# Attention and routed experts in one kernel: a new numbering of the expert arms, list scatters moved behind copies, one load of the first step, and small blocks that scatter without a copy

## The chip, the cores and the metric

The kernel runs on one core of a Trainium2 chip. The metric is device time in microseconds, from one launch to its end. Five engines work side by side: TensorE (PE; its weight loads are listed as PEld), VectorE (DVE), ScalarE (ACT), GpSimd (POOL) and SyncE (SP), the last of which mostly issues DMAs. Each has its own instruction stream, and they wait for each other by semaphores.

## The reference, cut to what matters

```python
# attention: 8 batches, 12 heads, 448 positions, 64 wide
scores = scale * np.matmul(q, k.transpose(0, 1, 3, 2)) - np.log(S)
attn = 1.0 / (1.0 + np.exp(-scores))
attn_out = np.matmul(attn, v)
x = attn_out.transpose(0, 2, 1, 3).reshape(B * S, H * D)      # 3584 x 768
# experts: only tokens with a positive skip score, one of 8 experts each
do_compute = x @ w_skip > 0
logits = x[do_compute] @ w_gate;  e_idx = argmax(logits)
y = gate_w * (relu(x @ w1[e]) @ w2[e])                        # 768 -> 1024 -> 768
out = x;  out[do_compute] += y
```

## The kernel before, in words

**Attention.** A step is one batch `b` and one pair of heads `hp`; there are 8 x 6 = 48 steps, and each has four chunks `c` of key positions. For a chunk PE makes scores (L217) into a PSUM tile of the tag s, of which there are two, ACT makes the sigmoid (L237) into a tile `at`, and PE multiplies with v (L245) into the PSUM tile `pa` of the step. PE's order is scores of chunk c, then values of chunk c − 2. The operands of the scores come from 32 x 32 block transposes on DVE (L202, `prep`). For those, a head pair's keys and queries lie in SBUF twice, the second time 32 rows lower and shifted by 32 columns. `load_kq` (L177) loads one such part by DMA, and `other_part` (L184) makes the second by copies on POOL, four for each two steps; they are in POOL's stream at c = 0 of each even step and fill the tiles of the two steps after it. The first step is special: `kq_first` is loaded in both parts, by eight DMAs from SP's and ACT's queues. PE multiplies an identity meanwhile (L594, `keep_busy`).

**Routing.** Three steps into a batch, the tokens of the batch before are assigned to experts, and a token's record is written to its expert's list in DRAM by an indirect DMA from POOL (L394), four per batch. They are kept in the list `due`, from which one is taken at set places in the order that is written out by hand: at steps hp = 3 after chunks 1 and 3, and at hp = 4 between and behind the copies of `other_part`. In the last batch two are taken at hp = 2, the others at hp = 3 after chunks 0 and 1. POOL also computes low parts of weights (L466) in the later batches.

**Experts.** Two blocks of 128 tokens of one expert are written out (`b0`, `b1`). Then a loop on the device (L1493) runs over the rest, with one kind of block each, read from a table. Two compares (L1482, L1483, L1488 in `choose`) lead into one of four arms: FULL (128 tokens), HALF (64), FEW (32) and SPLIT, which is FULL and splits the raw weights of the next expert into high and low parts on ACT and DVE besides. With these inputs the loop runs 14 times: SPLIT, HALF, FULL, HALF, FULL, then FEW and FULL twice, FEW, SPLIT, FEW, FULL, FEW. Each engine has the code of all four arms in its stream, one behind the other.

In FEW, a matmul has only 32 rows of output, so four quarters share PE: output half `o` (of two, 384 columns each) and inner half `m`. All four lie in one PSUM tile, `py`. ACT evicts those with m = 0 (L1400), DVE adds those with m = 1 (L1402). Then `put` has POOL test the sums (`seen`, L1253, which reads two elements), copy both halves from `yt` to `ys` (L1262), test again, and add the rows to the output by an indirect DMA (L550).

Of the kernel before, what the change touches and what calls it, by code (L numbers as in the profile page):

```python
# [10 lines left out]
F32 = mybir.dt.float32  # L11
# [8 lines left out]
P = 128  # L20
# [3 lines left out]
def kernel(  # L24
# [183 lines left out]
    def scores(b, hp, c, xs):  # L208

        sc = new_s(f"s_{b}_{hp}_{c}")
        for m in range(2):
            first, qs = (4 * m + c, slice(0, S)) if c < 3 else (3, slice(m * HQ, (m + 1) * HQ))
            for j in range(2):
                r = slice(j * D, (j + 1) * D)
                nc.tensor.matmul(  # L217
                    sc[m * D : (m + 1) * D, j, : qs.stop - qs.start],
                    xs[r, 0, first::NR7],
                    xs[r, 1, qs],  # L220
                    start=True,
                    stop=True,
                )
        return sc
# [346 lines left out]
    kq0 = wk.tile([P, 2, 1, NJ * D], F32, tag="xt", name="kq_first")  # L571
    for n in range(2):
        for h, eng in enumerate((nc.sync, nc.scalar)):
            load_kq(kq0, 0, 0, slice(0, 1), range(ND), (n,), (h,), eng)
    kq = {0: new_kq(0, 0)}
    load_kq(kq[0], 0, 0, slice(1, 2), range(1))

    warm = const.tile([P, 1], F32, name="warm")
    nc.scalar.activation(warm, bias, AF.Sigmoid)
    vs = {0: load_v(0, 0, 2)}  # L580
    kq[1] = new_kq(*steps[2])
    load_kq(kq[1], *steps[2], slice(0, 2), range(1))
# [62 lines left out]
    for n, (b, hp) in enumerate(steps):  # L645
# [39 lines left out]
        for c in range(4):  # L685
# [3 lines left out]
            if c == 0 and n % 2 == 0 and n + 2 < N:  # L689
                for g in range(2):  # L690
                    other_part(kq[n // 2 + 1], g)
                    if due and hp == 4 and b < B - 1:
                        due.pop(0)()
            if c == 0 and nxt:
                xs_next = prep(*nxt, part(n + 1)[0])
            done = next_values() if len(line) == 2 else None
# [32 lines left out]
                        wsplit(*w)  # L729


            if due and hp == 3 and (c % 2 if b < B - 1 else c < 2):
                due.pop(0)()

            if c == 3 and ready and not (hp == (3 if b < B - 1 else 2) and b > 0) or c == 1 and waiting:
# [263 lines left out]
    V.tensor_tensor(lnb, af, f_p, op=ALU.add)  # L999

    V.memset(f_hf, 0.0)
    V.tensor_scalar(f_last, f_last, 0.0, float(SPLIT), op0=ALU.is_gt, op1=ALU.mult)
# [245 lines left out]
    def put(n):  # L1248

        pool.tensor_tensor(rp[0], rid[:, 0:1], zero, op=ALU.add)  # L1250
        pool.tensor_tensor(rs, rp[0], zero, op=ALU.add)
        def seen(y, at):
            pool.tensor_tensor(  # L1253
                jk[:n], y[:n, at - 1 : at + 1], y[:n, at - 1 : at + 1], op=ALU.add
            )

        if n == SM:

            for o in range(2):
                seen(yt, (o + 1) * H2 - 1)  # L1260
                s = slice(o * H2, (o + 1) * H2)
                pool.tensor_copy(ys[:n, s], yt[:n, s])  # L1262
# [78 lines left out]
    def few(i):  # L1341
# [50 lines left out]
        for g in range(4):  # L1392
            load_w2(g, nx)
        for m in range(2):
            for o in range(2):
                g = 2 * o + m
                s = slice(o * H2, (o + 1) * H2)
                p = py[g * SM : (g + 1) * SM, 0, :H2]
                if not m:
                    nc.scalar.activation(yt[:SM, s], p, AF.Copy, scale=recs[:SM, 0, 0:1])  # L1400
                    continue
                nc.vector.scalar_tensor_tensor(  # L1402
                    yt[:SM, s], p, recs[:SM, 0, 0:1], yt[:SM, s], op0=ALU.mult, op1=ALU.add
                )
# [3 lines left out]
    def half(i):  # L1408
# [58 lines left out]
        advance()  # L1467

    arms = {
        FULL: lambda i: block(i, False),  # L1470
        SPLIT: lambda i: block(i, True),
        HALF: half,
        FEW: few,
    }
# [6 lines left out]
    def choose(kind, i):  # L1481
        with tc.If(kind < HALF) as c:  # L1482
            with tc.If(kind < FEW) as d:  # L1483
                run(FULL, i)
            with d.Else():
                run(FEW, i)
        with c.Else():
            with tc.If(kind < SPLIT) as d:  # L1488
                run(HALF, i)
            with d.Else():  # L1490
                run(SPLIT, i)

    with tc.For_i(0, nreg, 1, iteration_sync="reg_based") as i:  # L1493
        kind = entry(TYP, ds(i + 2, 1), mybir.ALL_ENGINES, SPLIT)
        choose(kind, i)


# [26 lines left out]
```

## Time and profile before

| | us |
|---|---|
| runs | 531.62, 535.46, 537.47 (median 535.46) |
| profiled execution | 538.86 |
| its span | 537.2 |
| PE busy | 506.3 |
| DVE busy | 296.9 |
| ACT busy | 274.0 |
| POOL busy | 259.5 |
| first scores on PE | 7.63 |
| loop's first matmul | 327.77 |
| last matmuls of the loop begin | 518.47 |
| last indirect DMA issued on POOL | 526.73 |

The profiled execution takes 1.66 us more than its span, and 3.4 us more than the median of the runs. The span falls into attention (to about 287 us), the routing's end with the two blocks written out (to about 325 us), and the loop. In the rows of the timeline stand the start, the length, the engine, the line, the operation with what it writes and reads, the count, and in brackets the idle time of the engine before it and what ended that. A "q" behind an engine's name is its sequencer, which reads instructions ahead of the engine's work and takes the branches.

### The profile page before, as it was taken

The numbers are of one execution on the slowest core, as the hardware profiler recorded it, in microseconds if no ns is written. First come the engines' busy times: TensorE is split into PE (matmuls) and PEld (weight loads), VectorE is DVE, ScalarE is ACT, GpSimd is POOL, SyncE is SP. The second block draws the span as 40 slices with busy tenths as digits, with TensorE's granted clock in tenths as the row PEclk, the third lists the DMA queues.
The fourth block names the chain that finished last, engine by engine and source line by source line (L and its number), as shares of the span: only waits on it lengthen the run. The fifth ranks groups of instructions, "written<-read, shape, count | busy, mean of one in ns | idle before, by whom it ended". The sixth has DMA issues, their size and how long they took to land.

```text
span 537.2 us, 15241 instructions
## 1 busy us (share of the span) xinstructions
PE 506.3 (94%) x4985; PEld 337.0 (63%) x4986; DVE 296.9 (55%) x732; ACT 274.0 (51%) x483; POOL 259.5 (48%) x413
## 2 busy tenths in 40 slices
PE   7999999999999999999999998999999999999970
PEld 5555555555555555556446986859587878787850
DVE  4555758568586795675856922962213232369321
ACT  3676766767767566666662122922212323177220
POOL 3523554345566874666674140453324444455642
PEclk8999999999999999999999998999999999999995
DMA  7999897798999899998964046688493959595930
GB/s 207 202 232 221 174 200 152 153 185 176 206 207 233 191 212 197 192 224 168 216 111 95 1 128 245 227 246 299 128 380 108 378 165 381 175 393 163 366 75 7
DMA packets 140481, 107.67 MB, mean 200 GB/s; under 512 B 97013, under 2 KB 112795, under 8 KB 140432
## 3 DMA queue, kind: packets, MB, share of 16 engines
q1 hardware_dynamic: 134096, 97.88, 70.0%
q0 software_dynamic: 4576, 8.66, 7.1%
q8 instruction: 31, 0.51, 0.4%
q10 hardware_dynamic: 1760, 0.48, 0.4%
q14 instruction: 18, 0.15, 0.1%
HBM read 98.93 MB, written 17.60 MB: 217 GB/s over the span
## 4 chain that ended last, share of the span: by engine, by line
PE 74%; DMA 9%; DVE 4%; SPq 4%; issue 3%; ACT 2%; POOL 1%; ACTq 0%; POOLq 0%; DVEq 0%
PE s L217 16%; PE pa L245 14%; PE ph L496 12%; PE py L523 11%; DMA out_dram<-y 4%; PE b_ph L496 3%; PE b_py L523 3%; PE py L1347 3%; PE ph L1347 3%; SPq L268 2%; PE pxt L472 2%; PE py L1414 2%; PE ph L1414 2%; DVE x L202 1%; DMA wr<-in_moe_w_dram 1%
## 5 line engine op out<-in xcount | busy, mean ns | idle before, releaser
L237 ACT ACTIVATE at<-s,bias 128x896 f32<-128x896 f32 x192 | 172.0, 914 | 84.6 <-PE s L217 82.3
L217 PE MATMUL s<-x 64*64 64x448 f32 (+1 forms) x1536 | 166.1, 501 | 7.0 <-DVE x L202 3.3
L245 PE MATMUL pa<-at,v 64*64 64x448 f32 (+1 forms) x1536 | 162.2, 490 | 0.0
L184 POOL COPY kq<-kq 32x896 f32<-32x896 f32 (+1 forms) x96 | 88.2, 919 | 104.6 <-DMA kq<-in_q_dram 62.0
L217 PEld LDWEIGHTS s<-x 64*64 64x64 f32 x1536 | 79.0, 191 | 63.7 <-issue 26.4
L245 PEld LDWEIGHTS pa<-at,v 64*64 64x64 f32 x1536 | 62.0, 133 | 55.7 <-issue 47.6
L202 DVE STREAM_TRANSPOSE x<-kq 128x448 f32<-128x448 f32 x94 | 83.0, 945 | 13.7 <-POOL kq L184 11.8
L255 DVE TENSOR_TENSOR xt<-xt,pa 128x448 f32<-128x448 f32 x48 | 29.5, 614 | 46.1 <-ACT xt L642 42.3
L394 POOL DMA_INDIRECT lst<-rec,idx x32 | 32.3, 1009 | 18.3 <-issue 10.5
L466 POOL TENSOR_TENSOR wl<-wr,wh 128x384 fp32r<-128x384 f32 (+1 forms) x28 | 31.7, 1143 | 8.9 <-DVE wh L465 7.7
L260 DVE STREAM_TRANSPOSE y<-xt 128x448 f32<-128x448 f32 x48 | 31.0, 646 | 4.4 <-DMA out_dram<-y 2.6
L550 POOL DMA_INDIRECT out_dram<-ys,rp x15 | 23.7, 1578 | 15.8 <-issue 8.2
L505 ACT ACTIVATE hs<-ph 128x512 f32<-128x512 f32 x14 | 8.4, 598 | 43.9 <-PE ph L496 35.9
L523 PE MATMUL py<-wh,hh 128*128 128x384 f32 x112 | 29.8, 346 | 0.0
L516 DVE TENSOR_TENSOR hl<-pht,hh 128x512 fp32r<-128x512 f32 x14 | 9.7, 690 | 36.0 <-ACT hh L515 27.6
L523 PE MATMUL py<-wh,hl 128*128 128x384 f32 x112 | 28.8, 338 | 0.0
L523 PE MATMUL py<-wl,hh 128*128 128x384 f32 x112 | 28.7, 337 | 0.0
L496 PE MATMUL ph<-wh,xh 128*128 128x512 f32 x84 | 26.3, 410 | 2.6 <-issue 2.6
L496 PE MATMUL ph<-wl,xh 128*128 128x512 f32 x84 | 27.2, 410 | 0.0
L482 DVE TENSOR_TENSOR xl<-pxt,xh 128x384 fp32r<-128x384 f32 x30 | 15.3, 552 | 20.7 <-PE py L1347 8.9
L642 ACT ACTIVATE xt<-pa 128x448 f32<-128x448 f32 x48 | 25.7, 536 | 1.9 <-PE pa L245 1.3
L496 PE MATMUL ph<-wh,xl 128*128 128x512 f32 x84 | 25.2, 404 | 0.0
(273 smaller groups left out, 666.9 us busy)
## 6 DMA issues: line engine op xcount, KB each, us to landing
raw<-in_moe_w_dram SPq DMA_DIRECT2D x64, 768.0 KB
v<-in_v_dram SPq DMA_DIRECT2D x48, 256.0 KB
out_dram<-y SPq DMA_DIRECT2D x192, 56.0 KB
kq<-in_k_dram SPq DMA_DIRECT2D x46, 224.0 KB
kq<-in_q_dram SPq DMA_DIRECT2D x46, 224.0 KB
wr<-in_moe_w_dram SPq DMA_DIRECT2D x12, 256.0 KB
wr<-in_moe_w_dram SPq DMA_DIRECT2D x16, 192.0 KB
lst<-fill SPq DMA_DIRECT2D x4, 464.0 KB
```

The costliest lines, as they stand in the source:

```text
L184: nc.gpsimd.tensor_copy(a[BT:, :, :, :BT], a[:BT, :, :, BT:])
L202: nc.vector.transpose(xs[:, n].rearrange("p (r j) -> p j r", j=NJ), t.rearrange("p (j d) -> p j d", d=D)[:, :, :BT],)
L217: nc.tensor.matmul(sc[m * D : (m + 1) * D, j, : qs.stop - qs.start], xs[r, 0, first::NR7], xs[r, 1, qs], start=True, stop=True,)
L237: nc.scalar.activation(at[:, :, :n], sc[:, :, :n], AF.Sigmoid, bias=bias, scale=SCALE)
L245: nc.tensor.matmul(pa[j * D : (j + 1) * D, r, qs], vt[rs, j, r + c if c < 3 else 3 * (1 - r), :], at[rs, j, : qs.stop - qs.start], start=( ...
L255: nc.vector.tensor_tensor(x, x, pa[:, 1, :S], op=ALU.add)
L260: nc.vector.transpose(y, xts[b][:, hp, :])
L394: put = nc.gpsimd.indirect_dma_start(out=lst[:, :], out_offset=bass.IndirectOffsetOnAxis(ap=idx[:, c : c + 1], axis=0), in_=rec[:, c, :], ...
L466: nc.gpsimd.tensor_tensor(lo, r, hi, op=ALU.subtract)
L496: nc.tensor.matmul(ph[h], a[:, j * P : (j + 1) * P], w[j][h], start=(n == 0), stop=(n == len(t) - 1),)
L523: last = nc.tensor.matmul(py[:, o, :H2], a[h][:, js], w[j][:, o * H2 : (o + 1) * H2], start=(j == 0 and n == 0), stop=(j == NK2 - 1 and n ...
L1347: nc.tensor.matmul(dst[g * SM : (g + 1) * SM, :n], a, w, start=(j == 0), stop=(j == most - 1), tile_position=(0, g * SM),)
```

## The change

Five edits:

1. The loads of `kq_first` fetch one part only (four DMAs of 32 x 896, where there were four more of 32 x 864). The second part is made by four copies, two on ACT and two on POOL, behind the warming sigmoid on ACT and ahead of the other copies on POOL. 
2. The third scores of the first step (0, 0, 2) go to a PSUM tile with the tag of `pa`, not to one of the two of the tag s.
3. In batches up to the last but one, list scatters are issued at hp = 3 after chunks 0 and 1 and at hp = 4 after chunks 1 and 2; none stands between or directly behind the copies of chunk 0 any more.
4. The arms are numbered SPLIT, FEW, HALF, FULL. The arm that the first compares lead into without a jump, and which stands first in the code, is SPLIT and no more FULL; SPLIT's old place has FULL.
5. In FEW the sums of half o = 0 lie in `py`, those of half o = 1 in the second tile of `pht`. The evictions go half by half, and `put` tests `yt` once and scatters from it.

```diff
+        if (b, hp, c) == (0, 0, 2):
+            sc = ps_a.tile([P, 2, 512], F32, tag="a", name="s_third")
+        else:
+            sc = new_s(f"s_{b}_{hp}_{c}")
...
-            load_kq(kq0, 0, 0, slice(0, 1), range(ND), (n,), (h,), eng)
+            load_kq(kq0, 0, 0, slice(0, 1), range(1), (n,), (h,), eng)
...
+    def first_part(n, h):
+        a = kq0[h * D : (h + 1) * D, n, 0].rearrange("p (j d) -> p j d", d=D)
+        return a[BT:, :, :BT], a[:BT, :, BT:]
+
+    for n in range(2):
+        nc.scalar.activation(*first_part(n, 1), AF.Copy)
+        nc.gpsimd.tensor_copy(*first_part(n, 0))
...
                 for g in range(2):
                     other_part(kq[n // 2 + 1], g)
-                    if due and hp == 4 and b < B - 1:
-                        due.pop(0)()
...
-            if due and hp == 3 and (c % 2 if b < B - 1 else c < 2):
+            if due and (c in (1, 2) and hp == 4 or c < 2 and hp == 3):
                 due.pop(0)()
...
-    FULL, FEW, HALF, SPLIT = range(4)
+    SPLIT, FEW, HALF, FULL = range(4)
...
-        if n == SM:
-
-            for o in range(2):
-                seen(yt, (o + 1) * H2 - 1)
-                s = slice(o * H2, (o + 1) * H2)
-                pool.tensor_copy(ys[:n, s], yt[:n, s])
-        seen(ys, H2)
-        out_rows = scatter(rp[0][:n], ys[:n], ALU.add)
+        y = yt if n == SM else ys
+        seen(y, H2)
+        out_rows = scatter(rp[0][:n], y[:n], ALU.add)
...
+        sums = (py[:, 0, :], pht[1])
...
-                    py[:, 0, :],
+                    sums[o],
...
-        for m in range(2):
-            for o in range(2):
+        for o in range(2):
+            for m in range(2):
                 g = 2 * o + m
                 s = slice(o * H2, (o + 1) * H2)
-                p = py[g * SM : (g + 1) * SM, 0, :H2]
+                p = sums[o][g * SM : (g + 1) * SM, :H2]
...
-                run(FULL, i)
+                run(SPLIT, i)
...
-            with tc.If(kind < SPLIT) as d:
+            with tc.If(kind < FULL) as d:
                 run(HALF, i)
             with d.Else():
-                run(SPLIT, i)
+                run(FULL, i)
```

How the instructions stand on POOL at the start; `kq_0` holds the second step (its numbers differ by the shorter list of instructions ahead):

```order
 L150 MEMSET tri_f 128x128
 L98 IOTA tok_i 32x1 x4
+L591 COPY kq_first<-kq_first 32x14x32
 L152 AFFINE_SELECT tri_f<-tri_f 128x128
-L184 COPY kq_0_180<-kq_0_180 32x14x32 x4
+L591 COPY kq_first<-kq_first 32x14x32
+L184 COPY kq_0_176<-kq_0_176 32x14x32 x4
 L184 COPY kq_2_190<-kq_2_190 32x2x14x32 x4
```

The two copies of the first step come ahead of the four of the second.

On POOL in the middle of batch 1, with what each instruction waits for (DMAHW: a load; DMASW: one of POOL's own indirect DMAs has landed). First before, where `kq_0` is filled at hp = 4 for the next batch's first two steps, and `kq_2` at that batch's hp = 0:

```order
L394 DMA lst<-rec_746,idx_858 29696x16
L184 COPY kq_0_860<-kq_0_860 32x2x14x32 [waits DMAHW4_49,DMAHW2_49]
L184 COPY kq_0_860<-kq_0_860 32x2x14x32 [waits DMAHW3_49,DMAHW5_49,DMASW1_49,DMASW0_49]
L394 DMA lst<-rec_746,idx_858 29696x16 [waits Pool_49]
L184 COPY kq_0_860<-kq_0_860 32x2x14x32
L184 COPY kq_0_860<-kq_0_860 32x2x14x32 [waits DMASW2_49]
L394 DMA lst<-rec_746,idx_858 29696x16 [waits Pool_49]
L184 COPY kq_2_996<-kq_2_996 32x2x14x32 [waits DMAHW2_49,DMAHW0_49,DVE_49]
L184 COPY kq_2_996<-kq_2_996 32x2x14x32 [waits DMAHW3_49,DMAHW1_49,DMASW3_49]
```

And now:

```order
L397 DMA lst<-rec_746,idx_858 29696x16
L184 COPY kq_0_860<-kq_0_860 32x2x14x32 [waits DMAHW6_49,DMAHW0_49]
L184 COPY kq_0_860<-kq_0_860 32x2x14x32 [waits DMAHW1_49,DMAHW7_49,DMASW1_49,DMASW0_49]
L184 COPY kq_0_860<-kq_0_860 32x2x14x32 x2
L397 DMA lst<-rec_746,idx_858 29696x16 [waits Pool_49]
L397 DMA lst<-rec_746,idx_858 29696x16
L184 COPY kq_2_996<-kq_2_996 32x2x14x32 [waits DMAHW6_49,DMAHW4_49,DVE_49]
L184 COPY kq_2_996<-kq_2_996 32x2x14x32 [waits DMAHW5_49,DMAHW7_49,DMASW3_49,DMASW2_49]
```

The third scatter has left its place among the copies: the last copy of `kq_0` waits for no landing, and the second copy of `kq_2` waits for two.

On ACT at the loop's entry, behind the two compares. Before, the first arm is FULL (its first instructions, and the branch at its end):

```order
L1482 COMPARE_AND_BRANCH
L1483 COMPARE_AND_BRANCH
L505 ACTIVATE hs_4026<-ph0_4442 128x512
L515 REGISTER_ALU
L515 ACTIVATE hh0_4419<-pht_4445 128x512
```

Now it is SPLIT, with the high parts of the weights (L1204) among the rest:

```order
L1488 COMPARE_AND_BRANCH
L1489 COMPARE_AND_BRANCH
L508 ACTIVATE hs_4026<-ph0_4442 128x512
L1204 ACTIVATE wh1_0_0_104<-raw1_0_0_4417 128x512
L1204 REGISTER_ALU
L1204 ACTIVATE wh1_1_0_106<-raw1_0_0_4417 128x512
```

SPLIT has moved from behind HALF to the front, on every engine, and FULL from the front to behind HALF; FEW stays last. An arm that isn't the last ends in a branch over those behind it.

More of the change, by code (lines that the diff above doesn't have):

```diff
@@ L208, in scores @@
     def scores(b, hp, c, xs):
-        sc = new_s(f"s_{b}_{hp}_{c}")
+        if (b, hp, c) == (0, 0, 2):
+            sc = ps_a.tile([P, 2, 512], F32, tag="a", name="s_third")
+        else:
+            sc = new_s(f"s_{b}_{hp}_{c}")
         for m in range(2):
@@ L1001 @@
     V.memset(f_hf, 0.0)
-    V.tensor_scalar(f_last, f_last, 0.0, float(SPLIT), op0=ALU.is_gt, op1=ALU.mult)
+    V.tensor_scalar(f_last, f_last, 0.0, float(FULL), op0=ALU.is_le, op1=ALU.mult)
     V.tensor_tensor(
@@ L1469 @@
     arms = {
+        SPLIT: lambda i: block(i, True),
         FULL: lambda i: block(i, False),
-        SPLIT: lambda i: block(i, True),
         HALF: half,
@@ L1487, in choose @@
         with c.Else():
-            with tc.If(kind < SPLIT) as d:
+            with tc.If(kind < FULL) as d:
                 run(HALF, i)
             with d.Else():
-                run(SPLIT, i)
+                run(FULL, i)
     with tc.For_i(0, nreg, 1, iteration_sync="reg_based") as i:
-        kind = entry(TYP, ds(i + 2, 1), mybir.ALL_ENGINES, SPLIT)
+        kind = entry(TYP, ds(i + 2, 1), mybir.ALL_ENGINES, FULL)
         choose(kind, i)
```

## The prediction

> **What bounds the kernel now.** I read the page's busy shares and chain first, then the clock and DMA share by stretch, then the three places where TensorE stands still for long: the start, the entry to the loop, the tail.
>
> ```profile
> PE 506.3 (94%) x4985; PEld 337.0 (63%) x4986; DVE 296.9 (55%) x732; ACT 274.0 (51%) x483; POOL 259.5 (48%) x413
> ...
> PE   7999999999999999999999998999999999999970
> ...
> PE 74%; DMA 9%; DVE 4%; SPq 4%; issue 3%; ACT 2%; POOL 1%; ACTq 0%; POOLq 0%; DVEq 0%
> ```
>
> TensorE is busy 94% of 537.2 us; about 31 us can be had from its idle time, and some more from a low clock. Nothing in the change shortens its matmuls. So each part is worth what it takes from PE's idle time, from a half-clock stretch, or from the ends where PE has not begun or has finished. The next view gives stretches: start and end, length, PE's busy time, granted clock, DMA share, GB/s (the first six also list the other engines).
>
> ```profile
> 9.00:10.00 1.00, 1.00 (x8) 0.09 (x4) 1.00 (x3) 0.86 (x1) 0.47 (x1) 0.50 1.23 235
> 11.00:12.00 1.00, 1.00 (x12) 0.49 (x8) 0.20 (x1) 0.51 (x2) 0.00 (x0) 0.58 1.01 240
> 100.00:150.00 50.00, 50.00 (x670) 27.19 (x666) 34.11 (x75) 34.98 (x46) 26.64 (x30) 1.00 0.92 185
> 150.00:200.00 50.00, 48.94 (x626) 26.93 (x621) 38.51 (x83) 34.53 (x46) 33.59 (x36) 1.00 0.97 209
> 200.00:250.00 50.00, 48.51 (x617) 28.58 (x613) 32.96 (x64) 34.27 (x45) 30.71 (x34) 1.00 0.93 194
> 250.00:287.00 37.00, 33.94 (x459) 18.73 (x451) 23.14 (x51) 22.01 (x31) 26.04 (x31) 1.00 0.83 173
> ...
> 327.70:329.00 1.30, 1.23 (x5) 1.00 1.05 364
> 329.00:332.70 3.70, 3.70 (x11) 0.54 1.03 365
> ```
>
> Attention until 150 us is PE without a gap, so time won at the start is carried. From 150 to 287 us PE loses 1.06, 1.49 and 3.06 us while the DMA engines are nearly full: there a lead can be lost again if the bytes don't come earlier too. The half clock shows at 9 to 12 us and at 329 to 332.7 us.
>
> **Part one, the start.** Rows: start, length, engine, line, operation, and the idle time before it.
>
> ```profile
> 1.53 4.14 PE L594 MATMUL idle<-ident 128*128 128x128 f32 x20 [1.53 <-POOL ident masks.py:199]
> 4.53 0.95 DVE L202 STREAM_TRANSPOSE x<-kq_first 128x448 f32<-128x448 f32 x1 [2.97 <-DMA kq_first<-in_k_dram]
> 6.64 0.94 DVE L202 STREAM_TRANSPOSE x<-kq_first 128x448 f32<-128x448 f32 x1 [1.17 <-DMA kq_first<-in_q_dram]
> 7.63 4.15 PE L217 MATMUL s<-x 64*64 64x448 f32 x24 [1.96 <-DVE ramp L601]
> 7.67 1.80 POOL L184 COPY kq<-kq 32x448 f32<-32x448 f32 x3 [0.34 <-DMA kq<-in_k_dram]
> 10.34 1.01 ACT L237 ACTIVATE at<-s,bias 128x896 f32<-128x896 f32 x1 [0.49 <-PE s L217]
> 11.30 0.50 PEld L245 LDWEIGHTS pa<-at,v 64*64 64x64 f32 x6 [0.26 <-DMA v<-in_v_dram]
> 11.54 1.08 PE L245 MATMUL pa<-at,v 64*64 64x448 f32 x8
> 11.84 1.01 ACT L237 ACTIVATE at<-s,bias 128x896 f32<-128x896 f32 x1 [0.49 <-PE s L217]
> ...
> L642 ACT ACTIVATE xt<-pa 128x448 f32<-128x448 f32 x48 | 25.7, 536 | 1.9 <-PE pa L245 1.3
> ```
>
> Removed: four loads of 32x864 words of 4 bytes, 0.44 MB. At the 235 GB/s of 9 to 10 us that is 1.9 us of all DMA engines. The keys' and queries' transposes wait for these loads (idle 2.97, 1.17). Added: four copies of 32x448. On POOL one takes 1.80 / 3 = 0.60 us; on ACT none of this shape was run, and its bounds are 0.54 (the row of the same length, on more partitions) and 1.01 (a sigmoid of twice the length); I take 0.54, the nearest. Both engines copy side by side, so about 0.6 us lies on the path for the queries; the keys' pair passes behind the queries' load. Queries ready: 6.64 − 1.9 + 0.6 = 5.3 us; transpose 0.94; first scores at about 6.3 instead of 7.63. That shrinks PE's gap after its warming matmuls (end 5.67) from 1.96 to about 0.6, so I expect the half clock of 8.4 to 11.8 to go. ACT's copies stand behind the table load and the warming sigmoid; DVE's transposes wait for them, and behind them on ACT stands only the first sigmoid, which needs the first scores anyway. POOL's stand ahead of the next step's copies, which waited 0.34 for their own load.
>
> The first values at 11.54 wait for v (0.26 at PEld). V's load stands behind the same queue; without 0.44 MB it lands 1.9 us sooner, near 9.4 to 9.6. Three scores at full clock need 3 x 0.75 = 2.25 (half of the 1.5 us from one sigmoid to the next, 10.34 to 11.84, at half clock), so to 8.6, with the third no longer waiting for a sigmoid's buffer. So v is last, PE waits about 0.9 for it, and the gain is **2.0**. Bounds: 0.9 if v's issue does not move with the first loads, 3.0 if v moves further and PE alone counts (11.54 − 8.6).
>
> **Part two, the list scatters.** Rows of POOL and DVE around the one place where a copy's wait reached PE, and two rows of sums over the run (total, times, longest).
>
> ```profile
> 207.98 0.36 DVE L465 CAST wh<-wr 128x384 fp32r<-128x384 f32 x1 [1.97 <-DMA wr<-in_moe_w_dram]
> 208.34 0.93 POOL L184 COPY kq<-kq 32x896 f32<-32x896 f32 x1 [3.04 <-DMA lst<-rec,idx]
> 209.30 1.72 DVE L202 STREAM_TRANSPOSE x<-kq 128x448 f32<-128x448 f32 x2 [0.96 <-DMA v<-in_v_dram]
> ...
> POOL kq L184 <- DMA lst<-rec,idx: 22.8, 13, 3.1
> ...
> PE s L217 <- DVE x L202: 3.3, 5, 1.2
> ```
>
> POOL's copies wait 22.8 us for scatters to land, but PE waited for a transpose only 3.3 us in all, 1.2 at most: the rest lies beside PE's work. With both even-step pairs of copies ahead of the second half of the scatters, the 208.34 copy would start about 3 us sooner. Yet DVE's cast, which waits for a weight load, ends at 208.34, so the transposes come at 208.4 and not at 209.3: 0.9 of the 1.2 are had there. The later scatters make the next even step's second copy wait instead. I take **0.6**, between 0 (that wait replaces this one) and 1.3.
>
> **Part three, the arms.** First the chain at the loop's entry, then the durations in ns of the compare-and-branch at the second test (least, median, greatest; first and last start), on ACT and on PE over the run and on PE from 340 to 352 us, and the row that follows the first SPLIT block.
>
> ```profile
> 322.07 3.16 PE b_py L523 x18
> 325.23 2.54 issue
> 327.77 8.08 PE ph L496 x27
> ...
> L1488 ACTq COMPARE_BRANCH  x8: 60/66/93, 323.7 to 488.2; - x8
> L1488 PEldq COMPARE_BRANCH  x8: 73/194/3435, 324.2 to 484.8; - x8
> ...
> L1488 PEldq COMPARE_BRANCH  x2: 73/136/198, 344.6 to 346.3; - x2
> ...
> 347.83 5.37 PE L1414 MATMUL ph<-raw,xf 128*64 128x512 f32 x24
> ```
>
> PE's sequencer took 3.44 us for its first jump, at 324.2, over two arms into SPLIT; the seven others took 0.07 to 0.2. ACT's jump took at most 0.09. The chain names no engine that PE waited for, so I read it as its code being fetched. PE stood still 2.54, and then lost 3.70 x (1 − 0.54) = 1.7 to the low clock. With SPLIT as the first arm the entry takes no jump, SPLIT's code follows what runs already, and 2.54 + 1.7 = 4.2 go.
>
> But SPLIT now ends in a jump over three arms to code that PE has not run. The sequencer runs ahead of the matmuls: before, it left SPLIT at 344.6, read the next kind of block and reached its last test at 346.3, while PE had work until 347.83. A fetch of 3.44 moves that 346.3 + 0.2 to 349.9 and leaves PE idle for about 2.0, once. That is as long as the gap of 1.96 which preceded the first half-clock stretch, so I count 1.7 more. Net 4.2 − 3.7 = **0.5**. Ends: 4.2 if the exit's code lies ready, −0.5 if its fetch takes a microsecond longer.
>
> The Trainium skill ("Runtime: NRT & Kernel Launch", Instruction fetch mechanics) says that fetching ahead is purely sequential and that a taken branch out of a window of two pages waits for a fetch. The 3.44 us agree and speak against this part; the short later branches over the same distance do not agree with a window of two pages. The Trainium skill ("TensorE: Matmul & The Clock Gate", the clock gate) lets the clock fall only after an idle window of about 3.4 us. The gaps of 1.96 and 2.54 with a half clock behind them differ from it; by the page the exit would cost no clock and this part would come to 2.2.
>
> **Part four, the small blocks.** PE's slices are 9 through the whole loop, FEW's included, so only the last block counts. The last block's rows:
>
> ```profile
> 522.63 1.17 ACT L1400 ACTIVATE yt<-py,recs 32x384 f32<-32x384 f32 x2 [2.52 <-PE py L1347]
> 523.84 1.26 DVE L1402 SCALAR_TENSOR_TENSOR yt<-py,recs,yt 32x384 f32<-32x384 f32 x2 [2.56 <-ACT yt L1400]
> ...
> 525.24 0.18 POOL L1253 TENSOR_TENSOR jk<-yt 32x2 f32<-32x2 f32 x1
> 525.38 0.49 POOL L1262 COPY ys<-yt 32x384 f32<-32x384 f32 x1
> 525.95 0.18 POOL L1253 TENSOR_TENSOR jk<-ys 32x2 f32<-32x2 f32 x1
> 526.73 1.41 POOL L550 DMA_INDIRECT out_dram<-ys,rp  x1 [0.60 <-issue]
> ```
>
> DVE waits for both of ACT's evictions and can now begin after the first, 1.17 / 2 = 0.6 earlier. One copy and one test drop behind DVE's last result: 525.95 − 525.24 = 0.7. Together **1.3** (0.7 if DVE still waits for both), with nothing put in their place: the scatter reads what the test has seen.
>
> **Sum.** 2.0 + 0.6 + 0.5 + 1.3 = 4.4. From the profiled execution's 538.86 (537.2 and 1.66 around it) that is 534.5; from the median of 535.46, which lies 3.4 below it, 531.1.
>
> **Rivals.** *Everything in the arms is won*: the exit's code was fetched ahead, or a shorter gap leaves the clock alone. For it: only one slow branch in the trace. Against: nothing has run there. Gain 4.4 + 3.7 = 8.1, 527.4; with the start's upper end, 526.4.
>
> *The lead is lost again*: the DMA engines at 0.92 to 0.97 from 100 to 250 us set attention's end, and the start gives 0.9, the scatters 0, the arms 0, the tail 1.3: 533.3. If the exit's fetch is paid again at the second SPLIT block, as a window of two pages would have it, another 3.7 is lost: from 4.4 that is 0.7, 534.8. Against: the removed bytes lead the queue, and the later jumps are short.
>
> *Slower*: the two scatters that now stand together behind the copies land late for the next even step, whose second copy waits for both. The place is once in each of seven batches, the price that of the wait at 208.34, 1.2 us of PE each: 7 x 1.2 = 8.4 lost against 3.8 from the other parts, 540.1. It decides once a pair of copies ends later than the two transposes (1.72) before the step's first scores. Against it: 13 such waits now, and one that reached PE with 1.2.
>
> **Numbers.** The bound of 1% is 5.4 us; the three runs spread over 1.1%, so less can't be told from no change by one measurement. Chances: my forecast 0.45 (531.1, give or take 2.5, of which 0.18 lies below 530.1); all of the arms 0.22; lead lost 0.23; slower 0.10, of which 0.06 beyond 540.8. So faster 0.40, the same 0.54, slower 0.06. The range runs from 526.0 (the first rival with its upper start) to 536.0 (the second with its double fetch and a microsecond of spread).
>
> **What would show it.** First scores near 6.3 and values near 9.5 with a clock of 1.00 around 10 us; no "issue" in the chain at the loop's entry; a long branch and about 2 us without matmuls behind the first SPLIT block, a half clock after it; one test between DVE's last sum and the last scatter. I am wrong if v still sets 11.5, if the exit shows no gap, or if PE waits for transposes more than 3.3 us in all.

## The result, and the profile after

The changed kernel is slower. Its median over 20 runs is 540.53 us (535.77 to 544.36), that of the kernel before 534.01 us (531.22 to 537.47, 20 runs as well). The ratio of after to before is 1.0108, with a 95% interval of 1.0086 to 1.0130; it leaves out the two longest runs of the changed kernel (543.89 and 544.36), which lie over 1.5% above its fastest. I had forecast 531.1 us, and a range up to 536.0.

The two profiled executions differ by less than the medians: 538.86 us before, which is 4.9 above that kernel's median of 20, and 540.19 after, which is 0.3 below its own. So the profiles show where time moved, and only the timed runs show how much. Starts in both profiles, in us:

| | before | after |
|---|---|---|
| DVE's last addition of attention (48th step) | 285.18 | 281.99 |
| loop's first matmul | 327.77 | 323.02 |
| second block's first matmul | 347.83 | 345.64 |
| last block's first matmul | 513.62 | 517.36 |
| end of the span | 537.16 | 538.47 |

The changed kernel enters the loop 4.75 us earlier: 2.2 are a lead from attention, the rest is the entry's gap that has gone. From there to the last block it takes 8.5 us more than before (194.34 against 185.85), and the tail gives 2.4 back. So these two profiles place the loss in the loop.

The page of after, first TensorE's busy time and the shares of the chain that ended last:

```profile
PE 505.7 (94%) x4985; PEld 347.2 (64%) x4986; DVE 299.6 (56%) x732; ACT 274.0 (51%) x485; POOL 253.9 (47%) x395
...
PE 65%; DMA 17%; DVE 6%; issue 4%; SPq 2%; POOL 2%; ACT 2%; ACTq 0%; POOLq 0%; DVEq 0%
```

PE's share of the chain fell from 74% to 65%, that of DMA rose from 9% to 17%. By line, 7% of the span is now `out_dram<-ys,rp`, an indirect DMA that is not among the lines that the page of before lists. Something now waits for transfers that did not before.

**The start did what was forecast, and more.** The timeline of after (start, length, engine, line, operation, and idle time before it):

```profile
4.63 0.57 ACT L590 ACTIVATE kq_first<-kq_first 32x448 f32<-32x448 f32 x1 [0.27 <-DMA kq_first<-in_q_dram]
6.29 1.79 PE L220 MATMUL s<-x 64*64 64x448 f32 x16 [0.43 <-DVE x L202]
8.66 0.92 PE L248 MATMUL pa<-at,v 64*64 64x448 f32 x6
```

The first scores come at 6.29 (forecast 6.3, before 7.63), the first values at 8.66 (before 11.54). ACT's copy takes 0.57 us (0.54 assumed). The clock stays at 1.00, as the 9 to 10 us row of the next view shows.

**The lead shrinks near 206 us, and comes back.** Stretches of after (start and end, length, busy time of the five engines, clock, DMA share, GB/s), and the rows at that place:

```profile
9.00:10.00 1.00, 1.00 (x18) 0.78 (x18) 0.62 (x1) 1.00 (x2) 0.00 (x0) 1.00 1.11 269
...
206.00:210.00 4.00, 0.74 (x8) 0.36 (x8) 3.67 (x5) 0.35 (x1) 3.56 (x5) 1.00 0.93 151
210.00:214.00 4.00, 4.00 (x32) 1.79 (x28) 2.90 (x4) 1.04 (x2) 3.85 (x4) 0.57 0.86 185
```

```profile
204.73 3.91 POOL L184 COPY kq<-kq 32x896 f32<-32x896 f32 x4 [4.87 <-DMA kq<-in_q_dram]
209.61 1.36 PE L220 MATMUL s<-x 64*64 64x448 f32 x8 [3.26 <-DVE x L202]
```

In this profile POOL does not wait there for a list scatter to land (3.04 us before), but for the queries' load, 4.87 us. Its copy began at 204.38 before and begins at 204.73 now, whatever the lead. PE waits 3.26 us where it waited 1.2, and the clock then falls: 0.57 over 4 us. At the addition that ends the 36th step the lead is gone (215.31 before, 215.44 now), but at the last step it is 3.2 us again (first row of the table). Nor does this wait come from the change alone: in the profiles of four runs below whose attention is that of the kernel before, PE waits 3.07 us here (the arms alone), 2.08 (the small blocks alone), 3.56 (two PSUM tiles) and 2.82 (another layout), the first three times with a half clock behind it.

**The entry to the loop is free, the exit from SPLIT is not.** The branch of PE's sequencer at the second test (L1489 now), and the row behind the first SPLIT block:

```profile
L1489 PEldq COMPARE_BRANCH  x9: 68/218/5132, 321.9 to 515.6; - x9
```

```profile
345.64 1.97 PE L1420 MATMUL ph<-raw,xf 128*64 128x512 f32 x6 [3.92 <-issue]
...
346.70:350.20 3.50, 3.50 (x11) 1.93 (x9) 1.89 (x4) 0.00 (x0) 0.69 (x1) 0.51 0.70 91
```

The longest branch was 3435 ns and is 5132 ns. PE stands still 3.92 us behind SPLIT, and 3.5 us at clock 0.51 follow.

That the branch waits for code can be seen in the DMA queue that the page lists as `q8 instruction`. First before, over its long branch (324.1 to 327.7 us); then after, over the first 2.7 us of its own (338.4 to 341.1), in which no packet of q8 starts, and over the whole of it (338.4 to 343.6). The q8 row gives packets, MB and share of the engines:

```profile
DMA packets 119, 0.26 MB, mean 72 GB/s; under 512 B 0, under 2 KB 0, under 8 KB 118
q8 instruction: 1, 0.02, 2.2%
```

```profile
DMA packets 323, 1.07 MB, mean 394 GB/s; under 512 B 27, under 2 KB 31, under 8 KB 323
...
q8 instruction: 1, 0.02, 1.3%
```

Each of the two branches has one packet of 16 KB in it and ends 1.5 and 1.3 us after that packet. After that, and one packet at 332.13 before, no packet of q8 comes until the loop's last matmuls have ended, and no later branch of PE takes over 0.4 us.

**The small blocks have a new wait.** Sums of waits of after, the evictions of the last FEW but one with the last scatter of all, and the chain near its end:

```profile
ACT yt L1406 <- DMA out_dram<-ys,rp: 28.5, 5, 7.7
...
PE pht L513 <- ACT hs L508: 4.7, 3, 2.3
```

```profile
502.80 0.57 ACT L1406 ACTIVATE yt<-py,recs 32x384 f32<-32x384 f32 x1 [7.75 <-DMA out_dram<-ys,rp]
503.39 0.57 ACT L1406 ACTIVATE yt<-pht,recs 32x384 f32<-32x384 f32 x1
504.49 0.60 ACT L508 ACTIVATE hs<-ph 128x512 f32<-128x512 f32 x1 [0.52 <-ACT yt L1406]
...
528.03 1.39 POOL L553 DMA_INDIRECT out_dram<-yt,rp  x1 [0.60 <-issue]
```

```profile
519.51 5.69 DMA out_dram<-ys,rp
525.22 0.04 ACTq L1406
525.26 0.05 issue
525.31 0.58 ACT yt L1406
```

All five evictions of FEW on ACT wait for an indirect DMA that scatters `ys`, which is that of the 128-token block before (ACT copies the sums out of PSUM; this is the eviction). Before, ACT's eviction waited for PE. Behind it in ACT's queue stands `hs` of the next block, for which PE waits: 4.7 us in three places, 2.3 at most. At the end of the program the chain itself runs through that DMA, 5.69 us from its issue.

The order of instructions, with their waits, shows the cause. Before and after, ACT's first eviction of FEW:

```
L1400 ACTIVATE yt<-py,recs 32x384 [waits PE_I-4475_own,DVE_I-4475_own,Pool_I-4475_own,DMASW3_49]
L1406 ACTIVATE yt<-py,recs 32x384 [waits DVE_I-4475_own,PE_I-4475_own,DMASW2_I-4475_own,Pool_I-4475_own,DMASW3_49]
```

`DMASW2_I-4475_own` is new: the landing of the loop's own indirect DMAs. Since the scatter reads `yt` itself, `yt` may be written again only when that scatter has landed; and by the trace the wait ends with the latest scatter of the loop, that of another arm. In the program as built, the scatters of all four arms count up this one semaphore, which fits.

### The profile page after: what moved, and what is told of

Read it like the earlier page. It is cut to its first block, busy times and chain, and to the rows that moved or that the text cites. A ratio compares the mean times of both kernels' runs of the same rounds, so it can differ in the third digit from the quotient of the medians.

```text
span 538.5 us, 15194 instructions
## 1 busy us (share of the span) xinstructions
PE 505.7 (94%) x4985; PEld 347.2 (64%) x4986; DVE 299.6 (56%) x732; ACT 274.0 (51%) x485; POOL 253.9 (47%) x395
## 3 DMA queue, kind: packets, MB, share of 16 engines
q0 software_dynamic: 4576, 8.66, 6.8%
## 4 chain that ended last, share of the span: by engine, by line
PE 65%; DMA 17%; DVE 6%; issue 4%; SPq 2%; POOL 2%; ACT 2%; ACTq 0%; POOLq 0%; DVEq 0%
PE s L220 17%; PE pa L248 16%; PE py L526 9%; DMA out_dram<-ys,rp 7%; PE ph L499 6%; PE b_ph L499 3%; PE b_py L526 3%; DMA wr<-in_moe_w_dram 3%; DMA raw<-in_moe_w_dram 3%; PE ph L1420 2%; DMA out_dram<-y 2%; PE py L1420 2%; DVE x L202 2%; PE pxt L475 1%; SPq L177 1%
## 5 line engine op out<-in xcount | busy, mean ns | idle before, releaser
L240 ACT ACTIVATE at<-s,bias 128x896 f32<-128x896 f32 (+1 forms) x191 | 170.8, 914 | 84.7 <-PE s L220 82.8
L220 PE MATMUL s<-x 64*64 64x448 f32 (+1 forms) x1528 | 168.9, 498 | 5.3 <-DVE x L202 5.1
L248 PE MATMUL pa<-at,v 64*64 64x448 f32 (+1 forms) x1536 | 167.5, 492 | 0.0
L220 PEld LDWEIGHTS s<-x 64*64 64x64 f32 x1528 | 84.0, 191 | 55.4 <-issue 21.4
L248 PEld LDWEIGHTS pa<-at,v 64*64 64x64 f32 x1536 | 68.4, 134 | 51.5 <-issue 39.9
L1287 DVE TENSOR_SCALAR ys<-py,recs 128x384 f32<-128x384 f32 (+1 forms) x18 | 10.4, 612 | 25.8 <-PE py L526 20.7
```

The lines of the kernel that those rows point to most:

```text
L220: nc.tensor.matmul(sc[m * D : (m + 1) * D, j, : qs.stop - qs.start], xs[r, 0, first::NR7], xs[r, 1, qs], start=True, stop=True,)
L240: nc.scalar.activation(at[:, :, :n], sc[:, :, :n], AF.Sigmoid, bias=bias, scale=SCALE)
L248: nc.tensor.matmul(pa[j * D : (j + 1) * D, r, qs], vt[rs, j, r + c if c < 3 else 3 * (1 - r), :], at[rs, j, : qs.stop - qs.start], start=( ...
```

## The experiments

Theory A: the scatter without a copy is the main loss, through ACT's new wait. Theory B: the code fetch has only moved from SPLIT's entry to its exit, where it costs as much or more. Theory C: the start's lead, or the moved list scatters, are lost in the full DMA engines. Each edit alone on the kernel before comes first. The runs of one group shared a chip; times of different groups are compared by their ratios to the kernel before, which ran beside each.

**The start alone**

```diff
+        if (b, hp, c) == (0, 0, 2):
+            sc = ps_a.tile([P, 2, 512], F32, tag="a", name="s_third")
...
-            load_kq(kq0, 0, 0, slice(0, 1), range(ND), (n,), (h,), eng)
+            load_kq(kq0, 0, 0, slice(0, 1), range(1), (n,), (h,), eng)
...
+        nc.scalar.activation(*first_part(n, 1), AF.Copy)
+        nc.gpsimd.tensor_copy(*first_part(n, 0))
```

> The kernel before with the start alone (first step loaded once, shifted part copied, third scores in a tile of their own). Theory A (the small blocks' scatter without a copy is what costs, since ACT's eviction now waits for a scatter to land; the lead of the start is kept): first values near 8.7 instead of 11.5 us, and the whole 2 to 3 us faster. Theory C (the lead of the start is lost in the full DMA engines around 200 us, where PE now waits longer and the clock falls): first values near 8.7 all the same, but the whole within 1 us of before, with a gap of 2 us or more before the scores near 206 us.

Measured: 536.74 us against 538.37, ratio 0.9984 (0.9959 to 1.0008). The two medians are 1.6 us apart, the ratio is worth 0.9. In the profile the additions that end the 21st step, the 31st and the last, first of before, then of this run:

```profile
129.19 0.62 DVE L255 TENSOR_TENSOR xt<-xt,pa 128x448 f32<-128x448 f32 x1 [0.48 <-ACT xt L642]
186.48 0.60 DVE L255 TENSOR_TENSOR xt<-xt,pa 128x448 f32<-128x448 f32 x1
285.18 0.62 DVE L255 TENSOR_TENSOR xt<-xt,pa 128x448 f32<-128x448 f32 x1 [2.36 <-ACT xt L642]
```

```profile
127.05 0.62 DVE L258 TENSOR_TENSOR xt<-xt,pa 128x448 f32<-128x448 f32 x1 [1.10 <-issue]
187.18 0.58 DVE L258 TENSOR_TENSOR xt<-xt,pa 128x448 f32<-128x448 f32 x1
283.18 0.62 DVE L258 TENSOR_TENSOR xt<-xt,pa 128x448 f32<-128x448 f32 x1 [2.13 <-ACT xt L654]
```

At 129 us the lead is 2.1, at 186 us it is gone (−0.7), and at the last step it is 2.0. The time is theory C's outcome (within 1 us of before), the profile is not: there is no gap of 2 us near 206, and the lead is not lost for good. The interval of the time holds 2 us faster as well (−0.4 to 2.2). One pair of profiles can't settle it: in five profiles with one and the same attention code (before, the arms, the small blocks, two PSUM tiles, another layout) the last addition begins anywhere from 280.34 to 287.93.

**The list scatters alone**

```diff
-                    if due and hp == 4 and b < B - 1:
-                        due.pop(0)()
...
-            if due and hp == 3 and (c % 2 if b < B - 1 else c < 2):
+            if due and (c in (1, 2) and hp == 4 or c < 2 and hp == 3):
```

> The kernel before with the list scatters moved, nothing else. Theory A: within 1 us of before. Theory C with the scatters as its cause: 1.5 to 4 us slower, and PE waits for transposes more than 5 us in all where before had 3.3.

Measured: ratio 1.0015 (0.9992 to 1.0039), 0.8 us. POOL's waits for a scatter to land shrink from 22.8 us to the first row below, and PE's for transposes from 3.3 to the second:

```profile
POOL kq L184 <- DMA lst<-rec,idx: 2.5, 2, 1.5
...
PE s L217 <- DVE x L202: 1.9, 3, 1.4
```

The edit does on POOL what it says, and it is worth nothing that can be measured, since those waits lay beside PE's work. So the scatters alone are not the cause of the loss.

**The arms alone**

```diff
-    FULL, FEW, HALF, SPLIT = range(4)
+    SPLIT, FEW, HALF, FULL = range(4)
```

with the branches and the table's constants that go with it, as in the change.

> The kernel before with the arms in the new order, nothing else. Theory B (the fetch is moved from SPLIT's entry to its exit and costs as much or more there): no gap at the loop's entry, one of 2 to 4 us behind the first SPLIT block with 3.4 us of half clock after it; the whole between 0.5 us faster and 2 us slower. If the exit cost nothing it would be 4 us faster. Theories A and C say nothing of it beyond that.

Measured: ratio 1.0032 (1.0008 to 1.0056), 1.7 us slower. The branch, and the first matmul behind SPLIT:

```profile
L1483 PEldq COMPARE_BRANCH  x9: 68/218/5145, 326.3 to 515.9; - x9
```

```profile
350.11 1.80 PE L1414 MATMUL ph<-raw,xf 128*64 128x512 f32 x5 [3.98 <-ACT wh L1200]
```

The gap is 3.98 us and the clock 0.63 over 350 to 354.6 us. (The row names an ACT instruction as what ended the gap. The same gap in the changed kernel, 3.92 us, has no such name, and here too PE's sequencer was in its branch, from 342.82 to 347.96.) Theory B holds.

**The small blocks alone**

```diff
-                s = slice(o * H2, (o + 1) * H2)
-                pool.tensor_copy(ys[:n, s], yt[:n, s])
-        seen(ys, H2)
-        out_rows = scatter(rp[0][:n], ys[:n], ALU.add)
+        y = yt if n == SM else ys
+        seen(y, H2)
+        out_rows = scatter(rp[0][:n], y[:n], ALU.add)
```

with `sums[o]` and the order of the evictions, as in the change.

> The kernel before with the small blocks' change alone (sums in two PSUM tiles, halves evicted in order, scatter without a copy). Theory A: 3 to 5 us slower, with gaps of about 1 to 2 us on PE in the blocks that follow a FEW block and ACT's evictions of FEW waiting for the landing of the scatter of the block before. If the copy was off every path, 1 us faster through the tail.

Measured: ratio 1.0024 (1.0001 to 1.0048), 1.3 us slower. The wait is there:

```profile
ACT yt L1396 <- DMA out_dram<-ys,rp: 17.7, 4, 8.0
```

Four evictions wait, 17.7 us in all, and PE stands still 2.19 at one of them (in the FULL block behind the second SPLIT and FEW), with 3.4 us of half clock behind it. The expected gaps in several places did not come here. The time is less than theory A's 3 to 5 us; the runs with the copy kept show why.

**The changed kernel with the copy kept**

```diff
-        y = yt if n == SM else ys
-        seen(y, H2)
-        out_rows = scatter(rp[0][:n], y[:n], ALU.add)
+        if n == SM:
+            for o in range(2):
+                seen(yt, (o + 1) * H2 - 1)
+                s = slice(o * H2, (o + 1) * H2)
+                pool.tensor_copy(ys[:n, s], yt[:n, s])
+        seen(ys, H2)
+        out_rows = scatter(rp[0][:n], ys[:n], ALU.add)
```

> The changed kernel with one thing undone: the small blocks copy their sums again before the scatter, as before, so that the scatter does not read what ACT evicts into. Theory A (the new wait of ACT's eviction for the scatter's landing costs): the gaps of 1.2, 1.2 and 2.3 us on PE behind FEW blocks go, ACT's wait for that landing (28.5 us in the changed kernel) goes from the sums of waits, and the time is 2 to 4 us below the changed kernel's, which means about 2 to 4 us above before. Rival (the gaps come from later weight loads or code, not from that wait): the gaps stay and the time is that of the changed kernel.

Measured: ratio 0.9974 (0.9945 to 1.0002), 1.3% below the changed kernel's 1.0108, which was measured apart from it (side by side it is 0.7%, below). I had expected it 2 to 4 us above before, and it is 1.4 below. The gaps behind FEW blocks are gone, and ACT's eviction waits for PE again:

```profile
ACT yt L1411 <- PE pht L1357: 5.8, 4, 1.5
```

**The kernel before with its halves in two PSUM tiles, copy kept**

```diff
+        sums = (py[:, 0, :], pht[1])
...
-        for m in range(2):
-            for o in range(2):
+        for o in range(2):
+            for m in range(2):
```

> The kernel before with the small blocks' halves in two PSUM tiles and evicted half by half, but still copied ahead of the scatter. Theory A: no new gap on PE, the tail 0.6 us shorter, the whole between 0 and 1 us faster. If the two tiles or the order of evictions cost something by themselves: as slow as the run with the small blocks' whole change, 1.3 us above before.

Measured: ratio 0.9953 (0.9931 to 0.9976), 2.5 us faster, more than expected. So the small blocks' change has a half that gains, 0.47%, and a half that loses: with the scatter uncopied it is 1.0024, with the copy 0.9953, 0.7% or 3.8 us between them, from two groups of runs.

**Another layout of the arms**

```diff
-    FULL, FEW, HALF, SPLIT = range(4)
+    FULL, FEW, SPLIT, HALF = range(4)
...
-        with tc.If(kind < HALF) as c:
+        with tc.If(kind < SPLIT) as c:
...
-            with tc.If(kind < SPLIT) as d:
-                run(HALF, i)
-            with d.Else():
-                run(SPLIT, i)
+            with tc.If(kind < HALF) as d:
+                run(SPLIT, i)
+            with d.Else():
+                run(HALF, i)
```

The code then stands as FULL, SPLIT, HALF, FEW.

> The kernel before with the arms laid out FULL, SPLIT, HALF, FEW, so that SPLIT begins in the 16 KB of code next to what runs at the loop's entry and ends in the 16 KB ahead of the loop's end. Theory B (code is fetched one 16 KB piece ahead, and the long branch is a fetch out of turn): no branch of PE's sequencer over 0.5 us, no gap at the entry and none behind the first SPLIT block, 2.5 to 4 us faster than before. Rival (the first jump into or out of an arm is slow wherever it goes): a gap of 2 us or more at the entry or behind SPLIT stays and the time is within 1 us of before.

Measured: 529.42 us against 534.41, ratio 0.9886 (0.9854 to 0.9918), 6.1 us faster by that ratio. The branch, and two stretches with PE's busy time, clock, DMA share and GB/s:

```profile
L1488 PEldq COMPARE_BRANCH  x8: 73/192/607, 320.6 to 475.3; - x8
```

```profile
320.00:325.00 5.00, 5.00 (x25) 1.00 0.43 124
325.00:345.00 20.00, 20.00 (x109) 1.00 0.79 291
```

No branch is above 0.61 us, and PE runs through the entry (321 us) and SPLIT's exit (the second block's first matmul is at 340.09) without a gap and at full clock. Nothing but the numbers of the arms and their place in the code was changed. The 16 KB packet is there again, but it starts at 335.06, ahead of the branch of 0.61 us at 336.85: the code fetched late is what cost, and that is avoidable on both sides. The 6.1 is more than the 4.2 that the entry took; the rest is not accounted for (the interval goes down to 4.4).

**The new start, the two PSUM tiles and that layout together**

> The kernel before with the new start, the two PSUM tiles with the copy kept, and the arms laid out FULL, SPLIT, HALF, FEW; the list scatters stay as before. If the parts add up: 0.9 from the start, 0.6 from the tail and 2.5 to 4 from the layout, 4 to 5.5 us faster than before. If they take from each other (the lead lost in the full DMA engines): 2.5 to 4 us faster.

Measured: 526.71 us against 534.41, ratio 0.9837 (0.9808 to 0.9866).

**Less to load in the middle of attention**

```diff
-                    vs[n // 2 + 1] = load_v(*steps[n + 2], 2)
+                    if 2 <= steps[n + 2][0] < 6:
+                        vs[n // 2 + 1] = vs[n // 2]
+                    else:
+                        vs[n // 2 + 1] = load_v(*steps[n + 2], 2)
```

once on the kernel before, once on the one with the new start.

> The kernel before without the v loads of batches 2 to 5: those steps multiply with the v tile that is there already, so the result differs, and about 0.5 MB of each 10.6 us are not moved between 60 and 220 us. It is the base for the next run. If DMA bandwidth makes PE's gaps from 150 to 220 us (theory C), they go here: 1 to 4 us faster than before at the end of attention. If not, they stay.

> The new start alone, again without the v loads of batches 2 to 5. Theory C (the start's lead is lost because the DMA engines are full): the lead of about 2.2 us over the run before this one is still there at 220 us, and the whole is 1.5 to 2.5 us faster than that run, where it was 0.9 with the loads in. Rival (the lead is lost in POOL's or DVE's work whatever the bytes): under 1 us again.

Measured: 740.7 us (740 because many more blocks follow, as other values route other tokens) and 736.5, ratios to the kernel before 1.3790 (1.3736 to 1.3844) and 1.3724 (1.3663 to 1.3785). Additions that end the same two steps (the 21st and the 36th), without and then with the new start:

```profile
131.03 0.62 DVE L255 TENSOR_TENSOR xt<-xt,pa 128x448 f32<-128x448 f32 x1 [0.74 <-ACT xt L642]
217.90 0.60 DVE L255 TENSOR_TENSOR xt<-xt,pa 128x448 f32<-128x448 f32 x1
```

```profile
126.80 0.62 DVE L258 TENSOR_TENSOR xt<-xt,pa 128x448 f32<-128x448 f32 x1 [0.77 <-ACT xt L654]
212.26 0.59 DVE L258 TENSOR_TENSOR xt<-xt,pa 128x448 f32<-128x448 f32 x1
```

The stretch from 150 to 200 us in the second of them, with the DMA share in the last column but one:

```profile
150.00:200.00 50.00, 48.76 (x630) 28.23 (x626) 39.19 (x83) 34.61 (x46) 34.47 (x34) 1.00 0.74 164
```

Here the lead is 4.2 at 131 us and 5.6 at 218 us, where the run with the loads in had lost it for a while by 186 us; the DMA share is 0.74 over this stretch, against 0.97 before. The medians end 4.2 apart. The direction is theory C's, and its rival (the lead lost whatever the bytes) doesn't fit these two profiles. But the size is more than the start gives, the two intervals overlap, and with the loads in the lead was 2.0 at the last step too. So that full DMA engines take the lead is not shown.

**The last layout with the list scatters moved, and with the scatter uncopied besides**

> The new start, the moved list scatters, the two PSUM tiles with the copy kept, and the arms laid out FULL, SPLIT, HALF, FEW. Against the run of the same without the moved scatters (ratio 0.984): the scatters' move is worth between 0.5 us faster and 1 us slower, so 0.983 to 0.986.

> The same as the run before this one, but scattering the small blocks' sums without a copy: the changed kernel with another layout of the arms. Theory A: 4 to 7 us slower than the run before this one (0.992 to 0.998 of before), with gaps on PE behind FEW blocks and ACT waiting for the scatter's landing. Rival (the direct scatter costs so much only beside the fetch at SPLIT's exit): within 1.5 us of the run before this one.

Measured: 0.9890 (0.9851 to 0.9930) and 0.9960 (0.9929 to 0.9990). The scatter without a copy costs 0.7% here too, 3.8 us, with ACT's wait of 18.0 us in four places and a gap of 2.67 on PE:

```profile
ACT yt L1406 <- DMA out_dram<-ys,rp: 18.0, 4, 8.5
```

So the scatter without a copy costs without the fetch at SPLIT's exit too. The first of the two is 0.5% above the run without the moved scatters, but on another chip; hence the last group, four kernels on one chip.

**Four on one chip:** the changed kernel; it with the copy kept; start, two tiles and the layout FULL, SPLIT, HALF, FEW; the same with the list scatters moved.

> The changed kernel, on one chip with the three runs behind it, since the earlier runs were spread over several. If it is as slow as first measured: ratio to before 1.007 to 1.014.

> The changed kernel with the copy ahead of the scatter kept. If the scatter without a copy costs the same beside the other edits as alone (0.7% between the two pairs of runs so far): 0.7% below the changed kernel. If it costs more beside the fetch at SPLIT's exit: 1.3% below it, as the runs on two chips had it.

> New start, two PSUM tiles with the copy kept, arms laid out FULL, SPLIT, HALF, FEW, list scatters as before. Ratio to before 0.982 to 0.987 if the first measurement holds on this chip.

> The same with the list scatters moved. If their move costs 0.5%, as two chips had it: 0.5% above the run before this one. If that was the chips: within 0.2% of it.

| kernel | us | ratio to before (537.11) | interval |
|---|---|---|---|
| changed | 542.88 | 1.0100 | 1.0067 to 1.0133 |
| changed, copy kept | 538.40 | 1.0028 | 1.0001 to 1.0056 |
| start, two tiles, layout | 531.06 | 0.9910 | 0.9876 to 0.9945 |
| the same, lists moved | 531.11 | 0.9889 | 0.9861 to 0.9918 |

The scatter without a copy costs 0.7% beside the other edits as well. The moved lists cost nothing. What the better version gains differs between chips, 1.6% on one and 0.9 to 1.1% on others; on each it is faster than the kernel before, which ran beside it. The second row and the fourth differ by the arms alone: SPLIT in front instead of FULL, SPLIT, HALF, FEW costs 7.3 us, the largest step between the changed kernel and the best.

How much the wait for the scatter costs can be read from the loop. In the first profile of the changed kernel PE had gaps of 1.18, 1.23 and 2.32 us behind FEW blocks, in the profile of its repeat one of 1.92 with a half clock behind it. Yet from the loop's first matmul to the last block's first matmul the repeat takes 194.6 us against 190.0 with the copy kept, and the last layout 188.7 uncopied against 184.2: 4.5 us both times. The tail gives 0.7 to 0.8 of that back.

One thing is still open. The four parts alone add up to −0.16 + 0.15 + 0.32 + 0.24 = 0.55%, each give or take 0.24, and the whole measures 1.0 to 1.1%. That is at the edge of what these intervals allow. In the loop the parts do add up: on the chip of the first group that same stretch takes 185.8 us with the lists alone, 190.2 with the arms and 189.7 with the small blocks, 4.4 and 3.9 more, and the changed kernel has 8.5 more than before. So the rest lies outside the loop, and no run shows a cause for it.

## Why the prediction was wrong

**Bounds (not shown to be wrong).** That the lead could be lost between 150 and 287 us was in the text, as a rival with 0.23. In the profiles it shrinks there and is back at the last step, 3.2 us in the changed kernel and 2.0 with the start alone. The wait near 206 us went from 1.2 to 3.3 us, but it is 2.1 to 3.6 in runs with the old attention too. The prediction took 1.2 from one profile as the size of that wait.

**The start (mechanism right).** Queries, first scores (6.29 for 6.3) and the half clock that goes came as said. V came sooner than the forecast: PE's weight load for the first values waited 0.35 us for a sigmoid, then 0.18 for v. So the first values came 2.9 us earlier, near the upper bound of 3.0 and not the 2.0 of the sum. The timed worth is 0.9 (−0.4 to 2.2), which leaves open whether "time won at the start is carried".

**The list scatters (wrong).** 0.6 was forecast, and the run alone shows 0.8 slower, give or take 1.3: nothing. The step that 0.9 of the 1.2 at 208 us can be had failed. With the scatters moved and nothing else, PE still waits 1.41 us for the transposes at that place, and in the changed kernel 3.26, where POOL waits for the queries' load until 204.73 and the transposes for the copies behind it. In all PE waits 5.1 us for transposes in the changed kernel, beyond the 3.3 that the prediction named as a sign of being wrong.

**The arms (right in kind, one term mis-sized).** No gap at the entry, one at the exit, half clock behind it: as forecast. The exit was put at 2.0 + 1.7 by the entry's 3.44 us; the branch took 5.13, the gap 3.92. With that gap the prediction's own sum is 4.2 − 5.6, or 1.4 slower. The forecast of 0.5 faster measured 1.7 slower (0.4 to 3.0). My end for that case, "a microsecond longer" and −0.5, was too near. The rival that everything in the arms is won was not what this layout did, but another layout did it.

The sentence by the Trainium skill ("Runtime: NRT & Kernel Launch", Instruction fetch mechanics), that a taken branch out of the window of prefetched code waits for a fetch, is what this trace shows: 3.44 and 5.13 us, each with one packet of 16 KB of the instruction queue inside it, and 0.61 at most where that packet came ahead of the branch. Its window of two pages isn't: in every kernel the later branches over the same distances took about 0.2 us.

**The small blocks (wrong: a wait was overlooked).** The step "with nothing put in their place: the scatter reads what the test has seen" failed. The copy was not only work; it let ACT write `yt` without regard to the scatter. From ACT's first eviction to the last indirect DMA the tail did shrink, from 522.63 to 526.73 (4.1 us) to 525.31 to 528.03 (2.7), the 1.3 of the forecast. But the eviction itself began later for the wait, and so did blocks in the loop: 1.3 us slower alone, where the same edit with the copy kept is 2.5 faster. It is the largest term that the sum lacked: 4.5 us in the loop, 3.8 with the tail. The sentence that only the last FEW block counts fell with it, since a stalled ACT holds the next block's `hs`.

**The rival on the slow side** had the list scatters as its cause. It gave 540.1 us, near the measured 540.5, by a mechanism that the runs don't show; that it came near is luck.

## What to carry to other kernels

A copy between a tile that an engine fills and a DMA that reads it also cuts a wait: before it is removed, ask who writes that tile next, what is queued behind that writer, and when the DMA lands. A wait of PE that one profile shows in a stretch with full DMA engines may be 1.2 us in one execution and 3.6 in the next with the same code there: look at several profiles before a gain is read from it, or a loss. And the order in which the arms of a branch stand in the code has a price, which these runs paid at the first jump to code that had not been fetched; where the arms were laid out so that the code of the first path came ahead of its branch, they did not pay it.

## What was not expected of the hardware

The longest branch took 3.0 to 3.4 us at the loop's entry and 5.06 to 5.15 behind SPLIT, in all kernels of either layout. The difference lies ahead of the 16 KB packet: it starts 0.60 to 0.65 us after the branch at the entry (five profiles), and 2.67 to 2.76 after it behind SPLIT (five profiles). In those 2.7 us the DMA engines move weights, at 394 GB/s in the changed kernel, against 72 GB/s over the entry's branch of before. That the packet stands behind these loads is likely, but no run varied it.

Whether a gap is followed by a half clock is not a matter of its length alone. Gaps of 1.96, 2.08 and 1.91 us were followed by one, gaps of 2.28 (the start alone, at the entry) and 2.82 (the layout FULL, SPLIT, HALF, FEW, from 207.6 us) were not. By the clock records of the traces each half-clock stretch within the work lasted 3.41 us (the row over 346.7 to 350.2 us above is one), and one, behind SPLIT in the repeat of the changed kernel, twice that: its row over 346 to 353.2 us has a clock of 0.53.

```profile
346.00:353.20 7.20, 5.45 (x14) 2.91 (x16) 4.72 (x10) 0.86 (x2) 2.42 (x2) 0.53 0.38 54
```
